# Two token tiles of a MoE layer through Strassen's seven block products

## The chip, the cores and the metric

The kernel runs on one core of a Trainium2 chip. The metric is the device time of one execution in microseconds (us). The engines are TensorE (PE, matrix products), VectorE (DVE), ScalarE (ACT), GpSimd (POOL) and SyncE (SP), whose queue starts nearly all DMAs. Each engine works off its own list of instructions in the order in which the program emits them, and waits on semaphores where an operand or a buffer is not ready.

## The reference

An attention-like read between `x` (4 batches, 8 heads, 512 positions, 64 wide) and a `state` of 32 rows gives 2176 tokens of 512 numbers. Two dense expert layers follow ("first" and "second MoE"); each is a product into 2048 columns, an activation, and a product back into 512.

```python
def _moe2_ref(x, w_in, w_out) -> np.ndarray:
    h = x @ w_in
    g = np.maximum(h, 0.0) + np.log1p(np.exp(-np.abs(h)))
    return (g @ w_out).astype(np.float32)
...
    x = np.ascontiguousarray(attn_out.transpose(0, 2, 1, 3)).reshape(B * S, H * D)
    x = _moe_ref(x=x, **moe_kwargs)
    return _moe2_ref(x=x, **moe2_kwargs)
```

## The kernel before

The weights come as fp64 and are rebuilt in fp32. Every operand of a large product is kept as two fp32r halves, hi and lo, and a product is three matmuls (`mm3`): hi·hi, hi·lo, lo·hi.

**Windows.** The program is a list of 136 windows, `wins`. One window is 128 of the 2048 hidden columns for one tile of tokens. Windows 0 to 67 are the first MoE. The second MoE has five tiles: windows 68 to 83 (tile 0, 512 tokens), 84 to 87 (tile 1, the 128 state tokens), 88 to 103 (tile 2), 104 to 119 (tile 3) and 120 to 135 (tile 4), the last three with 512 tokens each. `S0`, `T3`, `A0` and `start2` hold these numbers; `LAG` is 3.

**One window i of a 512-token tile.** On PE, `l1` makes 12 matmuls of 512 columns (4 blocks of the 512 input features, 3 matmuls each) into one of the two PSUM buffers called `l`; then `l2` makes 12 matmuls of window i-3, which add to the four banks `acc0` to `acc3`. On ACT, `act_open` takes the sum h of window i through Abs, Exp, Identity(+1) and Ln (L808 to L811), into the tiles `ta`, `tb`, `tl`, of which there are two each; `cut_hi` then makes the hi half `gth` of window i-1 (L85). On DVE, `close` makes three operations for window i-1 (L818, L819, L88; the first one reads h from PSUM again), and `cut_lo` makes its lo half `gtl` (L88).

**What sets the order.** `ORDER` is the order of these parts inside a window, written by hand. Work that does not belong to a window's own chain (loads, splits of tokens and weights) hangs on a window number and a kind: `when(i, kind, fn)` registers it, and `run(i, kind)` emits it at that place. SP's DMAs are in one queue in program order, and each waits in that queue for its buffers and data. `load_x2`/`split_x2` bring the tokens of a tile from DRAM (`xd`) and split them; `evac` copies the four finished banks of a tile out and stores them.

**Weights.** `Pair` loads, rebuilds and splits 256 columns of a weight matrix; `W3[p]` holds hi and lo of the second MoE's first layer for windows 2p and 2p+1 of each tile (p from 0 to 7), `W4` its second layer. All of them stay in SBUF through tiles 0 to 4.

Of the kernel before, what the change touches and what calls it, by code (L numbers as in the profile page):

```python
# [9 lines left out]
F32 = mybir.dt.float32  # L10
# [8 lines left out]
def fused_kernel(ctx: ExitStack, tc: tile.TileContext, x, state, w1, w2, w3, w4, out):  # L19
# [24 lines left out]
    LEAD = 14  # L44
    W_ = (8, 2, 2, 0, 8, 3)
# [31 lines left out]
    side = new(psum, [P, 2, 512], F32, "at")  # L77
    turn = [0]

# [197 lines left out]
    def load_state():  # L277
        st = new(base, [P, H, D], F32, "xs", 4)
# [35 lines left out]
    class Attn:  # L314
# [318 lines left out]
    A0 = T3 + NF  # L633

    acc = [None] * 4
# [14 lines left out]
    def load_x2(ti, k):  # L650
        t = new(base, [P, 512], F32, "xs", 4)
# [62 lines left out]
    def l2(w):  # L714
        gh, gl = w.g
        first, last = w.j == 0, w.j == w.n - 1
# [30 lines left out]
    def evac(w):  # L747
        if w.ph == 1 and w.tl == "s":
            t = new(base, [P, 512], F32, "xs", 4)
            copy(t, acc[0])  # L750

            def pe():
# [4 lines left out]
                def rest():  # L757
                    t2 = new(base, [P, 512], F32, "xs", 4)
# [8 lines left out]
        for i in range(n):  # L767
            t = new(base, [P, 512], F32, "xs", 4)
# [16 lines left out]
            else:  # L785
# [4 lines left out]
                else:  # L790
                    b, r = u
                    nc.sync.dma_start(out[b * T : b * T + S, :].rearrange("(p r) d -> p r d", r=R)[:, r, :], t)

    def act_open(w):
        c = w.cols
        w.a = new(base, [P, 512], F32, "ta", 2)[:, :c]
# [4 lines left out]
        else:  # L801
# [7 lines left out]
            nc.scalar.activation(w.a, w.a, AF.Exp, scale=-1.0)  # L809
            nc.scalar.activation(w.b, w.a, AF.Identity, bias=1.0)  # L810
            nc.scalar.activation(w.l, w.b, AF.Ln)  # L811

    def close(w):
# [3 lines left out]
        else:  # L817
# [3 lines left out]
            w.gv = w.l  # L821

# [147 lines left out]
    for ti in range(len(tiles2)):  # L970
# [16 lines left out]
    when(A0, "end", swap_left)

    with tc.manual_schedule():
# [63 lines left out]
        for i in range(NW + LAG + 1):  # L1053
# [6 lines left out]
            run(i, "start")  # L1060
            for what in ORDER[min(i, 4) + (i >= NF)]:
# [23 lines left out]
            run(i, "end")  # L1085
        pools["w_cm"].__exit__(None, None, None)
# [31 lines left out]
```

## Time and profile before

| what | value |
|---|---|
| time, median of 3 runs | 723.45 us (723.34 to 724.09) |
| span of the profiled execution | 721.8 us |
| time less span | 1.65 us (1.5 to 2.3) around the span, at start and end |
| PE | 711.2 us busy, 99% of the span, granted clock at full speed in all slices |
| ACT, DVE | 444.0 us (62%), 441.9 us (61%) |
| DMA | 56.36 MB in 58943 packets |

The profile is of one execution. The time of that execution itself is not listed apart from its span, so the row "time less span" is what the timed runs have beyond it. A busy share is an average over a program with several stages; the change lies in the second MoE, which takes the last half of the span.

### The profile page before, as it was taken

What the parts mean: (1) busy time and instruction counts of PE and PEld (TensorE: products, weight loads), DVE (VectorE), ACT (ScalarE), POOL (GpSimd) and SP (SyncE); (2) the same over time, 40 slices, a digit from 0 to 9 for tenths busy, and PEclk for the clock granted to TensorE, in tenths of its full rate; (3) what the DMA queues carried; (4) which work ended last, traced back from release to release, by engine and by line L of the source; (5) the groups of instructions that cost most, each with busy time, mean ns of one, the idle gap of its engine ahead of it and who ended that gap; (6) DMA issues with size and microseconds to landing.
All of it is one profiled execution on the core that took longest, in us unless ns stands there. A gap on an engine that the chain in (4) does not pass through costs nothing.

```text
span 721.8 us, 10193 instructions
## 1 busy us (share of the span) xinstructions
PE 711.2 (99%) x4014; PEld 575.1 (80%) x4014; DVE 441.9 (61%) x694; ACT 444.0 (62%) x730; POOL 18.3 (3%) x22
## 2 busy tenths in 40 slices
PE   8989999999999999999999999999999999999997
PEld 7667777777777887778888888888888888888886
DVE  5888884674774255776998756445555445544543
ACT  5876775555645356677878656555665556565553
POOL 1001300021000000000000000000000000000000
PEclk9999999999999999999999999999999999999999
DMA  9981007045150031353433001010002000010001
GB/s 327 388 298 58 1 27 150 3 81 95 74 161 1 1 115 64 130 174 118 172 120 132 30 30 59 20 54 1 1 1 97 21 0 1 0 59 1 0 1 58
DMA packets 58943, 56.36 MB, mean 78 GB/s; under 512 B 36880, under 2 KB 39824, under 8 KB 58896
## 3 DMA queue, kind: packets, MB, share of 16 engines
q1 hardware_dynamic: 58608, 55.46, 23.9%
q8 instruction: 31, 0.51, 0.3%
q10 hardware_dynamic: 288, 0.26, 0.1%
q14 instruction: 16, 0.13, 0.1%
HBM read 45.74 MB, written 9.96 MB: 77 GB/s over the span
## 4 chain that ended last, share of the span: by engine, by line
PE 92%; DMA 4%; DVE 2%; ACT 1%; SPq 1%; issue 1%; DVEq 0%
PE acc L638 17%; PE acc L639 16%; PE acc L640 16%; PE l L700 11%; PE l L638 9%; PE l L640 9%; PE l L639 9%; PE at L299 2%; PE l L685 2%; DMA wq<-in_moe_w_in_dram 2%; DMA wq<-in_moe_w_out_dram 1%; DMA ws<-in_moe_w_in_dram 1%; PE at L423 1%; SPq L215 0%; DVE w L161 0%
## 5 line engine op out<-in xcount | busy, mean ns | idle before, releaser
L88 DVE TENSOR_TENSOR gtl<-tl,gth 128x512 fp32r<-128x512 f32 x64 | 44.3, 692 | 144.0 <-ACT gth L85 143.9
L808 ACT ACTIVATE ta<-l 128x512 f32<-128x512 f32 x68 | 40.7, 598 | 132.2 <-PE l L640 132.2
L639 PE MATMUL acc<-gtl,wq 128*128 128x512 f32 x244 | 95.4, 391 | 1.6 <-DVE gtl L88 1.4
L638 PE MATMUL acc<-gth,wq 128*128 128x512 f32 x244 | 96.4, 395 | 0.0
L640 PE MATMUL acc<-gth,wq 128*128 128x512 f32 x244 | 95.1, 390 | 0.0
L88 DVE TENSOR_TENSOR gtl<-ta,gth 128x512 fp32r<-128x512 f32 x68 | 47.3, 696 | 71.2 <-ACT gth L85 71.2
L799 ACT ACTIVATE ta<-l 128x512 f32<-128x512 f32 x68 | 40.3, 592 | 44.5 <-PE l L700 29.1
L638 PE MATMUL acc<-wq,gth 128*128 128x512 f32 x152 | 59.2, 390 | 0.0
L640 PE MATMUL acc<-wq,gtl 128*128 128x512 f32 x152 | 59.2, 389 | 0.0
L639 PE MATMUL acc<-wq,gth 128*128 128x512 f32 x152 | 59.2, 389 | 0.0
L639 PEld LDWEIGHTS acc<-gtl,wq 128*128 128x128 f32 x244 | 45.8, 188 | 11.9 <-DVE gtl L88 2.9
L638 PEld LDWEIGHTS acc<-gth,wq 128*128 128x128 f32 x244 | 45.8, 188 | 11.7 <-issue 2.1
L640 PEld LDWEIGHTS acc<-gth,wq 128*128 128x128 f32 x244 | 45.8, 188 | 9.7
L638 PE MATMUL acc<-wh,gth 128*128 128x512 f32 x136 | 52.9, 389 | 0.0
L639 PE MATMUL acc<-wl,gth 128*128 128x512 f32 x136 | 52.9, 389 | 0.0
L640 PE MATMUL acc<-wh,gtl 128*128 128x512 f32 x136 | 52.9, 389 | 0.0
L88 DVE TENSOR_TENSOR tl<-tl,ta 128x512 f32<-128x512 f32 x68 | 47.0, 692 | 2.4
L85 ACT ACTIVATE gth<-ta 128x512 fp32r<-128x512 f32 x68 | 42.1, 618 | 8.1 <-DVE ta L815 8.1
L818 DVE SCALAR_TENSOR_TENSOR tl<-l,tl 128x512 f32<-128x512 f32 x68 | 46.5, 684 | 0.0
L819 DVE SCALAR_TENSOR_TENSOR ta<-tb,ta 128x512 f32<-128x512 f32 x68 | 46.4, 682 | 0.0
L815 DVE SCALAR_TENSOR_TENSOR ta<-ta,l 128x512 f32<-128x512 f32 x68 | 46.2, 680 | 0.2 <-ACT ta L800 0.2
L811 ACT ACTIVATE tl<-tb 128x512 f32<-128x512 f32 x68 | 43.0, 633 | 2.2
(187 smaller groups left out, 1486.3 us busy)
## 6 DMA issues: line engine op xcount, KB each, us to landing
ws<-in_moe_w_in_dram SPq DMA_DIRECT2D x20, 512.0 KB, 4.2
ws<-in_moe_w_out_dram SPq DMA_DIRECT2D x20, 512.0 KB, 4.1
wq<-in_moe_w_in_dram SPq DMA_DIRECT2D x12, 512.0 KB, 7.9
wq<-in_moe_w_out_dram SPq DMA_DIRECT2D x12, 512.0 KB, 9.8
xd<-xs SPq DMA_DIRECT2D x16, 256.0 KB, 3.0
xs<-xd SPq DMA_DIRECT2D x16, 256.0 KB, 3.9
out_dram<-xs SPq DMA_DIRECT2D x15, 256.0 KB, 2.6
x<-in_x_dram SPq DMA_DIRECT2D x12, 256.0 KB, 4.2
```

The lines of the kernel that those rows point to most:

```text
L85: nc.scalar.activation(dst, src, AF.Copy)
L88: eng.tensor_tensor(dst, a, b, op=ALU.subtract)
L638: nc.tensor.matmul(o, lh, rh, start=first, stop=False)
L639: nc.tensor.matmul(o, lh, rl, start=False, stop=False)
L640: nc.tensor.matmul(o, ll, rh, start=False, stop=last)
L700: nc.tensor.matmul(w.h, l[:, g, f], r[:, g, :], start=i == 0, stop=i == len(terms) - 1)
L799: nc.scalar.activation(w.a, w.hc, AF.Relu, bias=1.0)
L808: nc.scalar.activation(w.a, w.hc, AF.Abs)
L811: nc.scalar.activation(w.l, w.b, AF.Ln)
L815: nc.vector.scalar_tensor_tensor(w.a, w.a, 1.0, w.hc, op0=ALU.min, op1=ALU.max)
L818: nc.vector.scalar_tensor_tensor(w.l, w.hc, 0.0, w.l, op0=ALU.max, op1=ALU.add)
L819: nc.vector.scalar_tensor_tensor(w.a, w.b, 1.0, w.a, op0=ALU.subtract, op1=ALU.subtract)
```

## The change

The first layer of tiles 3 and 4 was 2 times 16 windows of 12 matmuls. It is now done jointly. For each p (256 hidden columns), the 512 features are cut in two halves, the 256 columns in two halves, and the 1024 tokens are tile 3 and tile 4: a product of 2 by 2 blocks. Strassen's method in Winograd's form makes the four block sums from seven block products (`product`, 6 matmuls of 512 columns each) and additions before and after.

**Sums of weights** (`c_*`). The rebuilt weights of each p are kept in DRAM (`w3f`, a store behind `Pair.conv`). From window 79 to 96 they are read back (`c_load`), DVE makes four sums (`c_sums`), ACT and DVE split them (`c_hi`, `c_lo`), and `c_put` stores them to a packed DRAM array `w3c`. In windows 84 to 91 `c_raw` copies the three unsummed blocks of p = 0 to 7 there, six DMAs for each p. `c_get` loads the seven left operands of one p, 1792 columns of hi and as many of lo.

**Sums of tokens** (`b_*`). `b_load` reads tiles 3 and 4 at window 88; `b_sum`, `b_hi`, `b_lo` make the seven right operands in windows 90 to 102, into the places of `W3[0]` to `W3[6]` as these fall free.

**Windows 104 to 119** take one p in two steps. The bank A holds products 1 and then 2, B holds 6, 5 and 3, D holds 7 and 4. `st_even` starts A, B, D, adds A's copy `s1` to B in PSUM, copies `u` from B and `s` from D, and ends with h of tile 3's even window in A. `st_odd` makes h of tile 4's odd window (`x.h`) and tile 3's odd window (`w.h`) as sums of a bank and a copy, and ends with h of tile 4's even window in B. Tile 3's windows get their second layer as before, three windows later. Tile 4's g goes to DRAM (`g_put`, `gbd`).

**Windows 120 to 135** (`st_last`) are tile 4's second layer alone, from g read back (`g_get`) and split two windows at a time (`two_cut`). The two banks that attention used (`side`) become `two0` and `two1` from window 92. Stores of tiles 2 and 3 go two blocks at a time.

```diff
 W_ = (8, 2, 2, 0, 8, 3)
+    XS = 4
...
-    side = new(psum, [P, 2, 512], F32, "at")
+    pa_cm = tc.tile_pool(name="pa", bufs=1, space=bass.MemoryType.PSUM, reuse_waits="tile")
+    side = new(pa_cm.__enter__(), [P, 2, 512], F32, "at")
...
             self.rebuild(flat(self.v)[:, c], self.raw[:, part * n * M : (part + 1) * n * M])
+            if self.kept is not None and part == parts - 1:
+                nc.sync.dma_start(self.kept, self.v)
...
-    def l2(w):
+    def l2(w, blocks=range(4)):
...
-        for i in range(NK if w.ph == 1 else w.cols // P):
+        for i in blocks:
             if first:
-                acc[i] = bank(f"acc{i}", 1)
+                if w.st < 2:
+                    acc[i] = bank(f"acc{i}", 1)
+                else:
+                    acc[i] = two_bank(i - 1) if i in (1, 2) else bank("l1", 2)
...
+    LEFT = {"11": 0, "12": 1, "22": 2, "s1": 3, "s2": 4, "s3": 5, "s4": 6}
+    PRODUCTS = {1: ("11", "11"), 2: ("12", "21"), 3: ("s4", "22"), 4: ("22", "t4"), 5: ("s1", "t1"), 6: ("s2", "t2"), 7: ("s3", "t3")}
...
+    def c_raw(p):
+        for h, t in enumerate(W3[p]):
+            v = f32(t).rearrange("p (q j e f) -> p e j q f", q=2, j=2, e=2)
+            d = w3c[p][:, h].rearrange("p m (q f) -> p m q f", q=2)
+            for j in range(2):
+                nc.sync.dma_start(d[:, j], v[:, 0, j])
+            nc.sync.dma_start(d[:, 2], v[:, 1, 1])
+
+    def c_sums(p):
+        a11, a12, a21, a22 = w3_parts(vals.pop(p))
+        t = sums[p] = new(base, [P, 1024], F32R, "cv", 2)
...
+        add(s1, a21, a22)
+        sub(nc.vector, s2, s1, a11)
+        sub(nc.vector, s3, a11, a21)
+        sub(nc.vector, s4, a12, s2)
...
+    def c_put(p):
+        for h, t in enumerate((cur["c"], sums.pop(p))):
+            nc.sync.dma_start(w3c[p][:, h, 3:].rearrange("p m f -> p (m f)"), f32(t))
...
+    def product(o, m, p):
+        a, b = PRODUCTS[m]
+        c = LEFT[a] * 256
+        (wh, wl), (xh, xl) = ([t[:, c : c + 256] for t in WC[p]]), XC[b]
+        for q in range(2):
+            f, s = slice(q * P, (q + 1) * P), slice(q * S, (q + 1) * S)
+            for k, (l, r) in enumerate(((wh, xh), (wh, xl), (wl, xh))):
+                nc.tensor.matmul(
+                    o, l[:, f], r[:, s], start=m in (1, 6, 7) and q == k == 0, stop=q == 1 and k == 2, skip_group_check=True
+                )
...
+    def g_put(w):
+        close(w)
+        nc.sync.dma_start(gbd[w.j], w.gv)
...
+    def st_even(i, u):
+        p = (i - SA) // 2
+        w, v, late = wins[i], wins[i - 1], wins[SB + 2 * p - 2] if p else None
+        cur["A"], cur["B"], cur["D"] = two_bank(0), bank("l1", 2), two_bank(1)
+        product(cur["A"], 1, p)
+        s1 = new(pools["w"][0], [P, 512], F32, "cs")
+        copy(s1, cur["A"])
+        if late:
+            act_open(v)
+        product(cur["B"], 6, p)
+        product(cur["D"], 7, p)
+        add(cur["B"], cur["B"], s1)
+        cur["u"] = xs()
+        copy(cur["u"], cur["B"])
+        cur["s"] = xs()
+        copy(cur["s"], cur["D"])
+        close(v)
+        st_cut(v)
+        if late:
+            act_open(late)
+        cur["late"] = late
+        l2(u)
+        if u.j == u.n - 1:
+            evac(u)
+        product(cur["A"], 2, p)
+        w.h = cur["A"]
+        act_open(w)
+
+    def st_odd(i, u):
+        p = (i - SA) // 2
+        w, v, x, late = wins[i], wins[i - 1], wins[SB + 2 * p + 1], cur["late"]
+        product(cur["B"], 5, p)
+        product(cur["D"], 4, p)
+        x.h, w.h = xs(), xs()
+        add(x.h, cur["B"], cur["s"])
+        add(w.h, cur["D"], cur["u"])
+        if late:
+            g_put(late)
+        act_open(x if i < SB - 1 else w)
+        close(v)
+        st_cut(v)
+        if i == SB - 1:
+            two_cut(0)
+        l2(u)
+        product(cur["B"], 3, p)
+        wins[SB + 2 * p].h = cur["B"]
+        if i < SB - 1:
+            g_put(x)
+        else:
+            close(w)
+            st_cut(w)
...
+    def st_last(i):
+        a, b = wins[SB - NF : SB], wins[SB:]
+        if i == SB:
+            act_open(b[NF - 2])
+            l2(a[13])
+            l2(a[14])
+            l2(b[0], range(3))
+            g_put(b[NF - 2])
+            act_open(b[NF - 1])
+            l2(b[1], range(3))
+            two_cut(1)
+            l2(a[15])
+            g_put(b[NF - 1])
+            evac(a[15])
+            for j in range(2):
+                l2(b[j], (3,))
+        elif i - SB < NF - 1:
+            j = i - SB + 1
+            if j % 2 == 0 and j + 2 < NF:
+                two_cut(j // 2 + 1)
+            l2(b[j])
+            if j == NF - 1:
+                evac(b[j])
...
+    T1 = start2[2]
+    C0 = start2[1] - 3
+    for p in range(NP):
+        when(C0 + 2 * p - 2, "load", lambda p=p: c_load(p))
+        when(C0 + 2 * p, "split", lambda p=p: c_sums(p))
+        when(C0 + 2 * p, "conv", lambda p=p: c_hi(p))
+        when(C0 + 2 * p + 1, "split", lambda p=p: c_lo(p))
+        when(C0 + 2 * p + 1, "load", lambda p=p: c_put(p))
+        when(start2[1] + p, "load", lambda p=p: c_raw(p))
+    for j in range(2):
+        when(T1, "load", lambda j=j: b_load(j))
...
+    for p in range(1, NP):
+        when(SA + 2 * p - 3, "load", lambda p=p: c_get(p))
+    for n in range(4):
+        when((SB - 3, SB - 2, SB - 1, SB)[n], "load", lambda n=n: g_get(n))
```

DVE in the windows of tile 3, before: the lo half of a window, `close` of the next one, and so on (`l_` is the bank with h).

```order
L88 TENSOR_TENSOR gtl_5127<-tl_5082,gth_5126 128x512
L818 SCALAR_TENSOR_TENSOR tl_5121<-l_882_5091,tl_5121 128x512
L819 SCALAR_TENSOR_TENSOR ta_5119<-tb_5120,ta_5119 128x512
L88 TENSOR_TENSOR tl_5121<-tl_5121,ta_5119 128x512
L88 TENSOR_TENSOR gtl_5166<-tl_5121,gth_5165 128x512
L818 SCALAR_TENSOR_TENSOR tl_5160<-l_888_5130,tl_5160 128x512
L819 SCALAR_TENSOR_TENSOR ta_5158<-tb_5159,ta_5158 128x512
L88 TENSOR_TENSOR tl_5160<-tl_5160,ta_5158 128x512
```

DVE in the odd step of p = 2 now (`l_972` is B, `two_973` D, `two_971` A, `xs_5485` x.h, `xs_5486` w.h, `l_940` the B of p = 1).

```order
L870 TENSOR_TENSOR xs_5485<-l_972_5400,xs_5432 128x512
L870 TENSOR_TENSOR xs_5486<-two_973_5401,xs_5430 128x512
L854 SCALAR_TENSOR_TENSOR tl_5443<-l_940_5254,tl_5443 128x512
L855 SCALAR_TENSOR_TENSOR ta_5441<-tb_5442,ta_5441 128x512
L93 TENSOR_TENSOR tl_5443<-tl_5443,ta_5441 128x512
L854 SCALAR_TENSOR_TENSOR tl_5468<-two_971_5399,tl_5468 128x512
L855 SCALAR_TENSOR_TENSOR ta_5466<-tb_5467,ta_5466 128x512
L93 TENSOR_TENSOR tl_5468<-tl_5468,ta_5466 128x512
L93 TENSOR_TENSOR gtl_5504<-tl_5468,gth_5503 128x512
L854 SCALAR_TENSOR_TENSOR tl_5495<-xs_5485,tl_5495 128x512
L855 SCALAR_TENSOR_TENSOR ta_5493<-tb_5494,ta_5493 128x512
L93 TENSOR_TENSOR tl_5495<-tl_5495,ta_5493 128x512
```

Where each h came straight from a bank, two additions and the closes of three windows now stand in a row; the close that reads A (`two_971`) is behind both additions and behind the close of `l_940`.

SP from the stores of tile 0 at window 87 on, before: the stores, those of tile 1, and the loads of tile 3.

```order
L792 DMA out_dram<-xs_4220 128x512
L792 DMA out_dram<-xs_4223 128x512
L792 DMA out_dram<-xs_4226 128x512
L792 DMA out_dram<-xs_4229 128x512
L789 DMA out_dram<-xs_4397 32x512 x4
L662 DMA xs_4745<-xd_9_81 128x512
L662 DMA xs_4747<-xd_9_81 128x512
L662 DMA xs_4788<-xd_9_81 128x512
L662 DMA xs_4790<-xd_9_81 128x512
```

SP in the same place now (`w3c` is the packed weight array, `wq`, `wh`, `wl` are W3, `tt` and `cv` the sums, `w3f` the kept weights, `xd` the tokens).

```order
L822 DMA out_dram<-xs_4328 128x512
L885 DMA w3c_23_98<-wq_585_3214 128x2x128 x2
L886 DMA w3c_23_98<-wq_585_3214 128x2x128
L885 DMA w3c_23_98<-wq_585_3214 128x2x128 x2
L886 DMA w3c_23_98<-wq_585_3214 128x2x128
L878 DMA cv_4375<-w3f_16_91 128x1024
L907 DMA w3c_23_98<-tt_4366 128x1024
L907 DMA w3c_23_98<-cv_4347 128x1024
L885 DMA w3c_24_99<-wh_618_3421 128x2x128 x2
L886 DMA w3c_24_99<-wh_618_3421 128x2x128
L885 DMA w3c_24_99<-wl_619_3422 128x2x128 x2
L886 DMA w3c_24_99<-wl_619_3422 128x2x128
L923 DMA ws_4429<-xd_10_85 128x2x512
```

Between the last store of tile 0 and the loads of tokens there are now the copies of W3 for p = 3 and 4, one reload of kept weights and the sums of p = 3; the reload of p = 5 and the sums of p = 4 come behind the tokens.

## Rows read from the trace of the kernel before

**Rows 1.** Chain that ended last, 560 to 722 us, by line.
```profile
by line: PE acc L640 17.4%; PE acc L638 17.4%; PE acc L639 17.3%; PE l L640 15.3%; PE l L638 15.1%; PE l L639 15.1%; DVE xs L776 0.3%; ACT xs L85 0.2%; issue 0.0%
```

**Rows 2.** Busy time per stretch: PE, PEld, DVE, ACT, POOL, clock, DMA share, GB/s.
```profile
560.00:580.00 20.00, 20.00 (x90) 16.57 (x89) 8.61 (x14) 12.06 (x20) 0.00 (x0) 1.00 0.03 12
680.00:700.00 20.00, 20.00 (x90) 16.54 (x89) 8.61 (x15) 11.83 (x20) 0.00 (x0) 1.00 0.00 1
```

**Rows 3.** Timeline of ACT, windows of tile 4: start, duration, line, operands.
```profile
619.93 0.60 ACT L808 ACTIVATE ta<-l 128x512 f32<-128x512 f32 x1 [2.33 <-PE l L640]
620.56 0.63 ACT L809 ACTIVATE ta<-ta 128x512 f32<-128x512 f32 x1
621.23 0.63 ACT L810 ACTIVATE tb<-ta 128x512 f32<-128x512 f32 x1
621.89 0.63 ACT L811 ACTIVATE tl<-tb 128x512 f32<-128x512 f32 x1
622.43 0.61 ACT L85 ACTIVATE gth<-tl 128x512 fp32r<-128x512 f32 x1
...
658.01 0.60 ACT L808 ACTIVATE ta<-l 128x512 f32<-128x512 f32 x1 [2.33 <-PE l L640]
```

**Rows 4.** Timeline of DVE in the same windows.
```profile
623.08 0.69 DVE L88 TENSOR_TENSOR gtl<-tl,gth 128x512 fp32r<-128x512 f32 x1 [2.83 <-ACT gth L85]
623.68 0.69 DVE L818 SCALAR_TENSOR_TENSOR tl<-l,tl 128x512 f32<-128x512 f32 x1
624.28 0.68 DVE L819 SCALAR_TENSOR_TENSOR ta<-tb,ta 128x512 f32<-128x512 f32 x1
625.00 0.69 DVE L88 TENSOR_TENSOR tl<-tl,ta 128x512 f32<-128x512 f32 x1
```

**Rows 5.** Waits of 560 to 722 us: total, times, longest.
```profile
DVE gtl L88 <- ACT gth L85: 76.2, 29, 2.8
```

**Rows 6.** ACT groups by line and form.
```profile
L85 ACT ACTIVATE wq<-cv 128x1024 fp32r<-128x1024 f32 x16 | 16.9, 1054 | 5.6 <-DVE cv L161 3.7 <-PE acc L640 1.9
L85 ACT ACTIVATE gh<-at 128x512 fp32r<-128x512 f32 x27 | 16.1, 597 | 27.2 <-PE at L299 23.2 <-PE l L700 2.5 <-DVE gl L88 1.6
```

**Rows 7.** DVE groups by line and form.
```profile
L88 DVE TENSOR_TENSOR gl<-at,gh 128x512 fp32r<-128x512 f32 x27 | 18.6, 690 | 22.6 <-ACT gh L85 22.4
...
L88 DVE TENSOR_TENSOR wl<-cv,wh 128x1024 fp32r<-128x1024 f32 x8 | 9.8, 1219 | 0.0
...
L88 DVE TENSOR_TENSOR gl<-acc,gh 128x256 fp32r<-128x256 f32 x2 | 0.8, 418 | 0.0
```

**Rows 8.** Timeline of ACT: first operation on the product of windows 84 and 91.
```profile
427.13 0.60 ACT L808 ACTIVATE ta<-l 128x512 f32<-128x512 f32 x1 [2.48 <-PE l L640]
...
467.61 0.60 ACT L808 ACTIVATE ta<-l 128x512 f32<-128x512 f32 x1 [1.84 <-PE l L640]
```

**Rows 9.** DMA issues: queue, count, KB each, median us from issue to landing.
```profile
xd<-xs SPq DMA_DIRECT2D x16, 256.0 KB, 3.0
...
out_dram<-xs SPq DMA_DIRECT2D x15, 256.0 KB, 2.6
...
zd<-xs SPq DMA_DIRECT2D x4, 256.0 KB, 2.0
```

**Rows 10.** Busy time per microsecond (last two columns DMA share, GB/s), four of them.
```profile
122.00:123.00 1.00, 1.00 (x61) 0.85 (x64) 0.98 (x3) 0.00 (x0) 0.00 (x0) 1.00 1.27 282
123.00:124.00 1.00, 1.00 (x24) 0.78 (x13) 0.58 (x1) 0.68 (x2) 0.00 (x0) 1.00 1.34 231
269.00:270.00 1.00, 1.00 (x7) 0.80 (x6) 0.26 (x1) 0.91 (x2) 0.00 (x0) 1.00 1.00 367
276.00:277.00 1.00, 1.00 (x6) 0.83 (x5) 1.00 (x2) 0.00 (x0) 0.00 (x0) 1.00 1.05 406
```

**Rows 11.** Packets that moved in 122 to 123 us.
```profile
DMA packets 1117, 0.28 MB, mean 282 GB/s; under 512 B 1117, under 2 KB 1117, under 8 KB 1117
```

**Rows 12.** Timeline of SP: start, time of the issues together, line, count.
```profile
108.31 11.38 SPq L233 DMA_DIRECT2D xs<-in_x_dram  x16
...
266.85 0.90 SPq L117 DMA_DIRECT2D ws<-in_moe_w_in_dram  x2
```

More of the change, by code (lines that the diff above doesn't have):

```diff
@@ L633, in fused_kernel @@
     A0 = T3 + NF
-    acc = [None] * 4
+    SA, SB = start2[3:]
+    accs = [[None] * 4 for _ in range(2)]
     def mm3(o, lh, ll, rh, rl, first, last):
@@ L821, in close @@
             w.gv = w.l
+    w3f = [new(dram, [P, 1024], F32, f"w3f{p}") for p in range(NP)]
+    w3c = [new(dram, [P, 2, 7, 256], F32, f"w3c{p}") for p in range(NP)]
+    gbd = [new(dram, [P, 512], F32, f"gbd{j}") for j in range(NF)]
+    vals, sums, XC, WC, cur = {}, {}, {}, {}, {}
+    KEEP3 = {}
+    LEFT = {"11": 0, "12": 1, "22": 2, "s1": 3, "s2": 4, "s3": 5, "s4": 6}
+    PRODUCTS = {1: ("11", "11"), 2: ("12", "21"), 3: ("s4", "22"), 4: ("22", "t4"), 5: ("s1", "t1"), 6: ("s2", "t2"), 7: ("s3", "t3")}
@@ new lines, in c_sums, with c_hi @@
+    def c_sums(p):
+        a11, a12, a21, a22 = w3_parts(vals.pop(p))
+        t = sums[p] = new(base, [P, 1024], F32R, "cv", 2)
+        s1, s2, s3, s4 = (f32(t)[:, 256 * m : 256 * (m + 1)].rearrange("p (q f) -> p q f", q=2) for m in range(4))
+        add(s1, a21, a22)
+        sub(nc.vector, s2, s1, a11)
+        sub(nc.vector, s3, a11, a21)
+        sub(nc.vector, s4, a12, s2)
+    def c_hi(p):
+        cur["c"] = new(pools["w"][0], [P, 1024], F32R, "tt")
+        copy(cur["c"], f32(sums[p]))
@@ new lines, in c_lo, with c_get @@
+    def c_lo(p):
+        lo = sums[p]
+        sub(nc.vector, lo, f32(lo), f32(cur["c"]))
+    def c_put(p):
+        for h, t in enumerate((cur["c"], sums.pop(p))):
+            nc.sync.dma_start(w3c[p][:, h, 3:].rearrange("p m f -> p (m f)"), f32(t))
+    def c_get(p, hs=(0, 1)):
+        for h in hs:
+            if p % 2:
+                t = new(pools["x"][0], [P, NK, 512], F32R, f"x2{h}")
+                t = t.rearrange("p k f -> p (k f)")[:, : 7 * 256]
+            else:
+                t = new(base, [P, 7 * 256], F32R, "ws", 2)
+            WC.setdefault(p, []).append(t)
+            nc.sync.dma_start(f32(t), w3c[p][:, h].rearrange("p m f -> p (m f)"))
@@ new lines, in b_hi, with b_lo @@
+    def b_hi(m, what):
+        src = cur["t"] if what[0] == "t" else cur[what]
+        XC[what] = room_for(*KEEP3[m].home)
+        hi, lo = (t.rearrange("p (q s) -> p q s", q=2) for t in XC[what])
+        copy(hi, src)
+        cur["x"] = lo, src, hi
+    def b_lo():
+        lo, src, hi = cur["x"]
+        sub(nc.vector, lo, src, f32(hi))
+    def product(o, m, p):
[8 more added lines that the diff above has]
+                )
@@ new lines, in xs, with g_get @@
+    def xs():
+        return new(base, [P, 512], F32, "xs", XS)
+    def g_put(w):
+        close(w)
+        nc.sync.dma_start(gbd[w.j], w.gv)
+    def g_get(n):
+        if n < 2:
+            t = new(base, [P, 2048], F32, "ws", 2)
+        else:
+            t = new(pools["x"][0], [P, NK, 512], F32, f"x2{n - 2}").rearrange("p k f -> p (k f)")
+        cur["g", n] = t
+        for j in range(4 * n, 4 * n + 4):
+            nc.sync.dma_start(t[:, (j - 4 * n) * 512 : (j - 4 * n + 1) * 512], gbd[j])
@@ new lines, in st_cut, with two_cut @@
+    def st_cut(w):
+        cut_hi(w)
+        cut_lo(w)
+    def two_cut(n):
+        hi, lo = room_for(*KEEP3[(7, 6, 0, 1, 2, 3, 4, 5)[n]].home)
+        w, x = wins[SB + 2 * n], wins[SB + 2 * n + 1]
+        o = (2 * n) % 4 * 512
+        src = cur["g", n // 2][:, o : o + 1024]
+        copy(hi, src)
+        sub(nc.vector, lo, src, f32(hi))
+        w.g, x.g = ([t[:, 512 * e : 512 * (e + 1)] for t in (hi, lo)] for e in range(2))
+    def st_last(i):
[21 more added lines that the diff above has]
+                evac(b[j])
@@ L969, in fused_kernel @@
     plan_hops(HW[3], lambda: a0.rest())
[L970 removed]
+    for ti in range(3):
         i0 = A0 - 4 if ti == 0 else start2[ti] - 3
@@ L1060, in fused_kernel @@
             run(i, "start")
+            if i >= SA:
+                if i < SB:
+                    (st_even, st_odd)[(i - SA) % 2](i, u)
+                else:
+                    st_last(i)
+                run(i, "load")
+                continue
             for what in ORDER[min(i, 4) + (i >= NF)]:
```

102 lines of the change are left out of this document (86 added, 16 removed).

## Prediction

> **What bounds the kernel now.** I read the chain that ended last first, then the busy times by stretch, then the timelines of single windows. From 560 us on, the chain is matmuls alone but for the last copies, with nothing put down to issue [rows 1]. PE is busy for 20.00 of 20.00 us at full clock, while ACT has about 12 us of work in 20 and DVE 8.6 [rows 2]. So in this stage a microsecond of PE work removed is a microsecond gained, until ACT, DVE or a DMA becomes late. The helpers are far ahead: DVE waits 2.8 us in each window for ACT, which waits for PE [rows 5]. The price of a matmul comes from ACT, whose first operation on a window's product follows PE: seven windows, from 619.93 to 658.01 us, are 38.08 us [rows 3], so one of 24 matmuls is 5.44 us and one matmul 0.2267 us.
>
> **What goes.** Tiles 3 and 4 had 384 matmuls in the first layer, and now have 8 times 42, or 336. All are 128 by 512 with operands in the same layout, and the second layer keeps its number. 48 times 0.2267 us is 10.88 us off PE. Eight copies and eight subtractions that split tile 3's and 4's tokens go too, off the path.
>
> **What a pair costs the helpers.** One p now takes PE 66 matmuls, 14.96 us. A full `act_open` is 2.50 us from its start to the next instruction's start, an ACT copy 0.6 [rows 3, 6]. A `close` lasts 2.01 us, an instruction that doesn't need the one before starts 0.60 us after it, and an operation from PSUM is 0.69 [rows 4, 7]. ACT has four opens, three copies and two hi halves: 10.0 + 1.8 + 1.2 = 13.0 us. DVE has four closes, three additions and two lo halves: 8.0 + 2.1 + 1.4 = 11.5 us. Both fit into 14.96, but with little over, so the order decides. No row has DVE writing into PSUM as the addition to B does. I take 0.69 from the operation that reads PSUM; the bounds are 0.6 and double that, and as copy `u` has over 2 us to spare before product 5 overwrites B, either end costs nothing.
>
> I laid out one pair on the three engines, each in its order, with these durations, from the pair's first matmul at 0. Products 1, 6 and 7 end at 4.08, the second layer at 6.80, products 2, 5 and 4 at 8.16, 9.52 and 10.88, the second layer at 13.60, product 3 at 14.96. Two loops could be longer than that.
>
> The first is bank A. Product 4's last column is out 0.16 us after its slot. Then come `w.h`'s addition (to 11.77), the close of the late window (to 13.70), and the first operation of the close that reads A (to 14.30). The next product 1 wants A at 14.96. About 0.6 us are to spare.
>
> The second goes through DRAM. The tiles `tl` are two, so the Ln for `x.h` waits until the late window's g has landed in `gbd`. From the end of that window's close: landing 2.0 (plus 0.04 to start it and as much to see it), Ln 0.63, hi and lo of A's window 1.2, close of `x` 1.9, addition to B 0.6, close of the odd window 2.05, its hi half 0.6, open of the next late window 2.6, its close 2.05. That is 13.7 us, so it returns with 1.3 us to spare. Its one uncertain price is the landing: 2.0 us for single stores of 256 KB, 2.6 and 3.0 for stores in fours [rows 9]. `gbd` stores go singly, so I take 2.0; up to 3.3 us there is no stall.
>
> `c_get` of 1.8 MB is issued about 5 us into a pair and is wanted at the next but one product 1, 10 us later. At the 367 to 406 GB/s of large pieces [rows 10] it takes 5 us and some two for the start. Hidden, with 3 us to spare; without that cover each microsecond counts.
>
> **The end.** Windows 120 to 135 have only second layers, 2.72 us each. By the same layout PE meets its third one 0.5 us before `two_cut(1)` is done, because two opens, a close and a split of 1024 columns (1.05 and 1.22 us [rows 6, 7]) stand in line: +0.5, and 1.1 if a landing is 2.6. The last copies and stores are the same.
>
> **The stage before, windows 79 to 104.** DVE gets about 2.7 us and ACT 1.05 more in two windows for weight sums, and 1.2 and 1.05 for token sums, against 2.8 us of waiting in each window. That is covered. The DMAs are not so clearly. Windows 84 to 91 last 40.48 us between the first and the last of their opens [rows 8] and one window more, 45.9 us. In them SP moves 6.3 MB of `c_raw`, 4.2 of sums, 2.1 of reloads, 2.1 of tokens and 1.3 of outputs, 16.0 MB or 349 GB/s. In windows 87 to 90 it is 9.4 MB in 22.3 us, 420 GB/s. Pieces of 2 KB and more went at 367 and 406 GB/s, pieces of 256 bytes at 231 to 282 with the engines full [rows 10, 11]; the `c_raw` pieces have 512 bytes, and SP's 0.45 us to issue a DMA of 256 pieces [rows 12] alone holds them to 291. At a mean of 350 the 9.4 MB take 27 us, so the queue falls 5 us behind. What is late then is the store of the sums of p = 4, issued in window 90, and with it DVE's `c_sums` of p = 5 in window 91, which reuses the buffer. Behind it on DVE stands the close of window 91, normally 1.2 us into window 92; the matmuls of window 93 need its bank, 4.2 us later. 5 less 4.2 is 0.8 us; the whole stage laid out gives 0 with 512-byte pieces at 310 GB/s, 1.1 at 280, 4.4 at 231. I take 0.5, nearer to the large pieces since SP's issue sets the pace; both ends stay in the range.
>
> The Trainium skill, "DMA: Bandwidth & Descriptors", section Specifications, names 512 bytes as the smallest transfer at line rate and about 358 GB/s as one core's share of HBM. By these two, as an estimate, the 9.4 MB would take 26 us and the loss would be near zero; the rows with 406 GB/s go over its limit.
>
> **The early stores `w3f`** stand on SP right behind a conversion whose buffer the next load was waiting for anyway, and ahead of that load by one issue of 0.45 us [rows 12]. Loads run windows ahead, so zero; nothing else moved ahead of window 79.
>
> **Sum.** 721.8 - 10.88 + 0.5 (DMA) + 0.5 (end) = 711.9 us of span. The runs last 1.65 us beyond the span at their median, so 713.6 us.
>
> **Rivals.** (a) The forecast, PE stays full but for 0 to 2.5 us: 712.4 to 715.
>
> (b) The DMA queue falls further behind in windows 87 to 92. With 512-byte pieces at 231 GB/s, the rate of 256-byte pieces, and the rest at 340, windows 93 and 95 start 6.5 us late in total: 719.1. For it speaks the demand of 420 GB/s; against it that these pieces are twice as long. Result 715 to 722.
>
> (c) The landing of `gbd` takes longer. From 3.3 us on, each pair pays the rest, and the end a little too: in the layout 3.2 us in all at 3.5, 6.7 at 4.0, which makes 715.8 and 719.3 before the DMA term. For it speaks 3.0 for stores in fours [rows 9] and the weight loads on the same engines; against it that the late window's store starts when these have landed. The Trainium skill, same page, section Latency and other measured facts, puts HBM access at 0.2 us on average and 2 us at high load; by it, as an estimate, a landing near 3.8 would be possible where loads are in flight, but by the layout none is. The trace before has no such store beside weight loads.
>
> (d) Slower: the same queue, but `c_raw` at 150 GB/s. The pieces are strided on the SBUF side, and the copies of 64 KB in pieces of 128 bytes took SP 0.71 us each [rows 12], 92 GB/s. At 0.71 us for 128 KB it would be 185 GB/s, and the loss 9.4 us. From about 165 GB/s on, the loss is over the gain of 10.9; at 150 it is 16 us, so 729. Against it: no row with pieces over 128 bytes is that slow.
>
> That the work does not shrink is excluded: the program holds 336 matmuls where 384 were.
>
> **Chances.** (a) 0.60, (b) 0.14, (c) 0.14, (d) 0.08, and 0.04 for several together that land near the old time. 0.2%, or 1.4 us, is about what a measurement of this kernel can tell from no change. Faster: (a), and (b) and (c) but for 0.04, so 0.84. Slower: (d) and a little of the mixed cases, 0.10. Same: 0.06. The likeliest case alone has 712.4 to 715. The range starts at 712.2, no stall at all, and goes to 719.5, the prices worked out for (b) and (c); beyond it lie (d), the mixed cases and the far parts of (b) and (c), under 2 in 10.
>
> **What would show it.** Right: 336 matmuls at 0.227 us each in the new line; PE full in the Strassen stage, with no wait for DVE over 0.5 us at product 1; `gbd` landings near 2 us; a short wait or none at the first matmul of window 93. Wrong: waits of product 1 in every pair on the close that reads A, with ACT's Ln of `x.h` waiting for a DMA (c); DVE's `c_sums` of p = 5 waiting for several microseconds on DMA and PE idle at windows 93 and 95 (b, d); or an operation that writes PSUM from DVE that is much longer than 0.7 us.

## The result, and the profile after

The changed kernel takes 716.99 us at the median (715.87 to 717.69 in 4 runs), beside 723.77 (723.34 to 724.41) for the kernel before in the same session: a ratio of 0.9902, 95% interval 0.9888 to 0.9916, faster by 1.0%. The forecast was 713.6, the likeliest case 712.4 to 715, the range 712.2 to 719.5. The profiled execution took 716.87 us with a span of 714.7, that is 7.1 less than the span of before. One execution of an experiment, the first profile of `put_pool`, ran at a granted clock of 0.655 throughout; its trace isn't used, and `put_pool_b` gives that kernel's trace.

The page's busy times, and its line on DMA: 48 matmuls fewer, 9.5 us less PE time (up to window 0 it has 0.7 us more in this execution, with the same 147 matmuls), 102.5 MB moved where it was 56.4.

```profile
PE 701.7 (98%) x3966; PEld 566.4 (79%) x3966; DVE 484.7 (68%) x753; ACT 465.7 (65%) x753; POOL 18.3 (3%) x22
...
DMA packets 82880, 102.51 MB, mean 143 GB/s; under 512 B 38800, under 2 KB 54032, under 8 KB 82832
```

Two stretches in the Strassen stage and after it, busy times as in [rows 2]: PE is as full as before.

```profile
560.00:580.00 20.00, 20.00 (x90) 16.54 (x90) 14.20 (x23) 17.18 (x30) 0.00 (x0) 1.00 0.58 224
680.00:700.00 20.00, 20.00 (x90) 16.57 (x89) 2.82 (x3) 2.12 (x2) 0.00 (x0) 1.00 0.11 38
```

DVE went from 8.6 to 14.2 us in 20 and ACT from 12.1 to 17.2, and PE still waits for neither. The waits of PE between 430 and 712 us (total, times, longest) are two, and both lie before the Strassen stage:

```profile
PE l L653 <- DVE tl L854: 1.6, 1, 1.6
PE acc L653 <- ACT xs L90: 0.6, 1, 0.6
```

To see where the 7.1 us come from I follow ACT's first operation on a window's product, as in [rows 8]. Kernel before, windows 0 and 103:

```profile
20.51 0.60 ACT L799 ACTIVATE ta<-l 128x512 f32<-128x512 f32 x1 [0.40 <-PE l L700]
...
532.89 0.60 ACT L808 ACTIVATE ta<-l 128x512 f32<-128x512 f32 x1 [2.33 <-PE l L640]
```

Kernel after, windows 0, 84 and 103:

```profile
21.37 0.60 ACT L833 ACTIVATE ta<-l 128x512 f32<-128x512 f32 x1 [0.39 <-PE l L715]
...
427.93 0.60 ACT L842 ACTIVATE ta<-l 128x512 f32<-128x512 f32 x1 [1.53 <-PE l L655]
...
536.45 0.60 ACT L842 ACTIVATE ta<-l 128x512 f32<-128x512 f32 x1 [1.38 <-PE l L655]
```

Window 0 opens 0.86 us later than before. From window 84 to window 103 it is 105.76 us before (427.13 [rows 8] to 532.89) and 108.52 after: **2.76 us lost in the windows that now carry the extra transfers**. From window 0's open to the last matmul's start (717.43 before, 710.29 after) it is 696.92 and 688.92, 8.00 less: 10.88 for 48 matmuls, less 2.76, and 0.12 for all else. So 721.8 + 0.86 - 8.00 = 714.66, and the rest to 714.7 is the tail.

The 0.86 at the start is no part of the change: up to window 78 PE, ACT and DVE have the same instructions in all kernels below, and their profiles open window 0 anywhere between 20.34 and 21.64 us. The time beyond the span is 2.07 to 2.17 us in the four runs of the change. In the runs of the kernel before that stand beside the experiments it is 1.74 to 1.86, and in those of `raw_four_earlier` 1.78 to 1.87. Why is open.

The lost 2.76 us on DVE, the close of window 90 (its last row first), then `c_sums` of p = 5, then the close of window 91:

```profile
468.04 0.69 DVE L93 TENSOR_TENSOR tl<-tl,ta 128x512 f32<-128x512 f32 x1
475.05 0.43 DVE L870 TENSOR_TENSOR cv<-cv 128x256 f32<-128x256 f32 x1 [6.31 <-DMA w3c<-cv]
...
478.25 0.68 DVE L854 SCALAR_TENSOR_TENSOR tl<-l,tl 128x512 f32<-128x512 f32 x1
```

The same place on PE: the first second-layer matmul of window 91's slot, and the first matmul of window 93.

```profile
468.96 0.50 PE L653 MATMUL acc<-wh,gth 128*128 128x512 f32 x1 [0.59 <-ACT xs L90]
...
479.00 0.50 PE L653 MATMUL l<-x,wq 128*128 128x512 f32 x1 [1.58 <-DVE tl L854]
```

`c_sums` writes into the buffer whose store `c_put` of p = 4 is still under way. It waits 6.31 us, the close of window 91 stands behind it, and window 93 needs the bank that this close reads. That is the chain of the prediction's DMA term, with a gap of 1.74 us between the matmuls where the prediction took 0.5. The prediction didn't name the wait of 0.59 (a gap of 0.74): ACT's copy of tile 1's accumulator stands behind the hi half of the token block "22", whose tokens land late. After each of the two gaps the next six matmuls take 0.14 us more than usual; 0.74, 1.74 and twice 0.14 are the 2.76.

ACT there, the hi half of "22" and the copy behind it:

```profile
467.37 1.06 ACT L90 ACTIVATE wh<-ws 128x1024 fp32r<-128x1024 f32 x1 [1.28 <-DMA ws<-xd]
468.33 0.58 ACT L90 ACTIVATE xs<-acc 128x512 f32<-128x512 f32 x1
```

SP's queue, with `c_put` of p = 2 (two stores, the second needs DVE's `c_lo`) and of p = 4:

```profile
438.31 0.33 SPq L907 DMA_DIRECT2D w3c<-tt  x1
442.35 0.32 SPq L907 DMA_DIRECT2D w3c<-cv  x1
442.72 0.43 SPq L885 DMA_DIRECT2D w3c<-wq  x1
...
469.06 0.33 SPq L907 DMA_DIRECT2D w3c<-tt  x1
470.32 0.33 SPq L907 DMA_DIRECT2D w3c<-cv  x1
```

Busy times of two stretches; the last two columns are DMA share and GB/s:

```profile
435.00:442.70 7.70, 7.70 (x51) 6.91 (x50) 6.25 (x11) 6.19 (x10) 0.00 (x0) 1.00 0.59 187
445.00:467.00 22.00, 22.00 (x105) 18.29 (x104) 16.05 (x28) 14.24 (x22) 0.00 (x0) 1.00 1.02 305
```

From 445 to 467 us the engines are full at 305 GB/s, and the sums of p = 4, which DVE had finished at 464.4, leave SP at 470.3, and DVE goes on at 475.05, when they have landed. Before that SP stands for 3.7 us (438.64 to 442.35) at the head of its queue, waiting for DVE, with `c_raw` ready behind it and the engines 0.59 busy.

### The profile page after: what moved, and what is told of

It reads as the page before. It is cut to its first block, busy times and chain, and to the rows that moved or that the text cites. A ratio compares the mean times of both kernels' runs of the same rounds, so it can differ in the third digit from the quotient of the medians.

```text
span 714.7 us, 10383 instructions
## 1 busy us (share of the span) xinstructions
PE 701.7 (98%) x3966; PEld 566.4 (79%) x3966; DVE 484.7 (68%) x753; ACT 465.7 (65%) x753; POOL 18.3 (3%) x22
## 4 chain that ended last, share of the span: by engine, by line
PE 88%; DMA 6%; DVE 2%; ACT 1%; SPq 1%; issue 1%; DVEq 0%
PE acc L653 14%; PE acc L654 14%; PE acc L655 14%; PE l L715 11%; PE two L959 6%; PE l L653 5%; PE l L655 5%; PE l L654 5%; PE l L959 5%; PE at L313 2%; PE l L700 2%; DMA wq<-in_moe_w_in_dram 2%; DMA wq<-in_moe_w_out_dram 1%; DMA cv<-w3f 1%; DMA ws<-in_moe_w_in_dram 1%; PE two L653 1%
## 5 line engine op out<-in xcount | busy, mean ns | idle before, releaser
L833 ACT ACTIVATE ta<-l 128x512 f32<-128x512 f32 x68 | 40.2, 591 | 44.7 <-PE l L715 29.3
L93 DVE TENSOR_TENSOR gtl<-tl,gth 128x512 fp32r<-128x512 f32 x48 | 33.2, 691 | 41.6 <-ACT gth L90 41.4
L842 ACT ACTIVATE ta<-l 128x512 f32<-128x512 f32 x44 | 26.1, 594 | 40.8 <-PE l L655 40.8
L653 PE MATMUL acc<-wq,gth 128*128 128x512 f32 x120 | 46.8, 390 | 0.0
L655 PE MATMUL acc<-wq,gtl 128*128 128x512 f32 x120 | 46.7, 389 | 0.0
L654 PE MATMUL acc<-wq,gth 128*128 128x512 f32 x120 | 46.7, 389 | 0.0
L846 ACT ACTIVATE tb<-ta 128x512 f32<-128x512 f32 x68 | 43.1, 633 | 2.2
L834 ACT ACTIVATE ta<-ta 128x512 f32<-128x512 f32 x68 | 43.0, 633 | 2.2
L843 ACT ACTIVATE ta<-ta 128x512 f32<-128x512 f32 x68 | 43.0, 633 | 2.2
L653 PE MATMUL acc<-wh,gth 128*128 128x512 f32 x104 | 40.6, 390 | 0.6 <-ACT xs L90 0.6
```

The source lines that it names most:

```text
L93: eng.tensor_tensor(dst, a, b, op=ALU.subtract)
L653: nc.tensor.matmul(o, lh, rh, start=first, stop=False)
L654: nc.tensor.matmul(o, lh, rl, start=False, stop=False)
L655: nc.tensor.matmul(o, ll, rh, start=False, stop=last)
L834: nc.scalar.activation(w.a, w.a, AF.Square, scale=0.5)
```

## Experiments

**Theory 1**: 48 matmuls are 10.9 us, the Strassen stage has no loss, and what is lost is lost in windows 84 to 92, where the store of the sums of p = 4 lands late. Its rivals are in each expectation. The column "lost" is, in each run's profile, the time from window 84's to window 103's open, less the 105.76 us of before.

| kernel | median us | ratio to before, 95% | lost, us |
|---|---|---|---|
| the change | 716.99 | 0.9902 (0.9888 to 0.9916) | 2.76 |
| `raw_spread` | 713.83 | 0.9860 (0.9844 to 0.9876) | 0.01 |
| `raw_four_earlier` | 713.72 | 0.9852 (0.9836 to 0.9868) | 0.01 |
| `put_pool` | 714.02 to 714.95 | 0.9868 (0.9852 to 0.9885) | 0.01 (`put_pool_b`) |
| `tokens_first_put_pool` | 714.59 | 0.9867 (0.9853 to 0.9880) | 0.01 |
| `raw2_first` | 715.32 | 0.9881 (0.9864 to 0.9897) | 1.64 |
| `tokens_first` | 719.64 | 0.9931 (0.9917 to 0.9945) | 6.28 |
| `prod7_twice` | 728.06 | 1.0053 (1.0038 to 1.0068) | 4.08 |
| `dve_two_more_b` | 723.64 | 0.9994 (0.9985 to 1.0003) | 4.23 |
| `gbd_four_stores` | 731.98 | 1.0111 (1.0097 to 1.0125) | 4.11 |

The last three have the changed kernel's code in those windows, so the same code lost between 2.8 and 4.2 us there in four profiles, one of each kernel.

**Fewer bytes at a time: `raw_spread`.**

```
-        when(start2[1] + p, "load", lambda p=p: c_raw(p))
+        when(start2[1] + 2 * p, "load", lambda p=p: c_raw(p))
```

> The copies c_raw(p) leave in window 84+2p, no longer 84+p; nothing else differs from the changed kernel. Theory 1 (c_raw overfills the DMA engines in windows 84 to 91, so the store of the sums of p = 4 and the token loads land late): DVE's c_sums of p = 5 waits under 1 us, PE has no wait at windows 91 and 93, the open of window 96 comes 27.2 us after that of window 91 (now 29.6), and the time falls by 2.3 to 2.8 us, to 714.2 to 714.7. Rival (the delay comes from the token loads and the sums' own round trips, whatever c_raw does): the wait at window 93 stays over 1 us and the time within 0.7 us of 717.

The loss is gone. Busy times of 425 to 480 us here (the changed kernel has 52.84 us of PE there):

```profile
425.00:480.00 55.00, 55.00 (x294) 47.37 (x294) 41.72 (x68) 38.94 (x62) 0.00 (x0) 1.00 0.86 283
```

At 713.83 us it is 0.4% faster than the change, a little more than expected. `c_sums` still waits for DMA, 2.6 us at most (2.5 for p = 5, where under 1 was expected), which its two windows cover.

**As dense, but sooner: `raw_four_earlier`.**

```
-        when(start2[1] + p, "load", lambda p=p: c_raw(p))
+        when(start2[1] + p - 4, "load", lambda p=p: c_raw(p))
```

> The copies c_raw(p) leave in window 80+p instead of 84+p: still one per window, but gone before the tokens and the outputs of tile 1 come. Theory 1c (one c_raw per window with the sums is 289 GB/s, which fits; what overfills the queue is that 3.4 MB of tokens and outputs come in the same windows, 88 to 91): no PE wait from window 91 to 96, 714 to 714.6. Rival (c_raw in every window is too dense wherever it stands, since the sums' stores go round once in two windows behind it): PE waits of over 1 us somewhere in windows 82 to 92, 715.5 or more.

713.72 us, and PE is full in the same stretch:

```profile
425.00:480.00 55.00, 55.00 (x297) 47.50 (x296) 42.12 (x70) 38.91 (x62) 0.00 (x0) 1.00 0.90 297
```

One `c_raw` per window fits, if the tokens and the outputs of tile 1 don't come in the same windows.

**Another queue: `put_pool` and `put_pool_b`.** The sixteen stores `c_put` are issued by POOL, which is idle there; all bytes stay in their windows.

```
-            nc.sync.dma_start(w3c[p][:, h, 3:].rearrange("p m f -> p (m f)"), f32(t))
+            nc.gpsimd.dma_start(w3c[p][:, h, 3:].rearrange("p m f -> p (m f)"), f32(t))
```

> The stores c_put of the weight sums are issued by POOL, not behind the other DMAs on SP; c_raw stays where it is. Theory 1a (the store of p = 4 is late because it stands behind c_raw in SP's queue): it goes out some 4 us earlier, DVE's c_sums of p = 5 waits under 2 us, PE's wait of 1.6 us at window 93 goes and the one of 0.6 at window 91 stays: 1.7 to 2.0 us faster than the changed kernel, 715. Theory 1b (the 16 DMA engines are full, and the place in a queue makes no difference): the store lands as late as before, and the time stays within 0.7 us of 717.

> The stores of the weight sums on POOL once more, for a profile at full clock. Theory 1a: PE waits only at window 91, by 0.6 to 1.6 us, for ACT's copy that stands behind the tokens; none at window 93. If window 93 still waits, the place in SP's queue was not the cause there.

Theory 1a holds, and more came back than it said: window 91's wait went too, since the token loads no longer queue behind stores that wait for DVE. The two stretches of `put_pool_b`:

```profile
435.00:442.70 7.70, 7.70 (x51) 6.89 (x50) 6.30 (x11) 6.25 (x10) 0.56 (x2) 1.00 0.88 261
445.00:467.00 22.00, 22.00 (x105) 18.29 (x104) 15.97 (x28) 15.10 (x24) 2.13 (x4) 1.00 1.03 332
```

Beside the rows of the changed kernel: where SP stood waiting, 261 GB/s flow in place of 187. Over 425 to 480 us it is 312 GB/s against 298. So the bytes do fit; they didn't fit in one queue in that order. The Trainium skill, "DMA: Bandwidth & Descriptors", section Rules for kernel authors, says that spreading DMAs over issuing engines doesn't help bandwidth and only saves issue time. Here it gave 0.3% of the time. I put that down to the order: transfers no longer stand behind a store that waits for data, nor that store behind them. It isn't the rate of a second queue, as far as the runs tell: `raw_four_earlier`, with SP alone, moves 338 GB/s from 445 to 467 us at a share of 1.03, and `put_pool_b` 332. The stretches hold different transfers.

**Tokens first: `tokens_first` and `tokens_first_put_pool`.** The loop that registers `b_load` moves ahead of the one for the weights, so in window 88 the tokens are issued first.

```
+    for j in range(2):
+        when(T1, "load", lambda j=j: b_load(j))
     for p in range(NP):
         when(C0 + 2 * p - 2, "load", lambda p=p: c_load(p))
...
-    for j in range(2):
-        when(T1, "load", lambda j=j: b_load(j))
```

> The four loads of tokens (b_load) go to the front of window 88's transfers, ahead of the sums and of c_raw of p = 4; all else as in the changed kernel. Theory 1b (what stands ahead of the store of the sums of p = 4 in SP's queue sets when that lands, and with it window 93): PE's wait of 0.6 us at window 91 goes, since ACT has its tokens in time, but the same bytes still stand ahead of that store, so the wait at window 93 grows by as much: within 0.5 us of the changed kernel, 717. Rival (the two waits are separate losses): 0.7 us faster, 716.2.

> Both: token loads first in window 88, and the stores of the weight sums issued by POOL; c_raw stays as dense as in the changed kernel. Theory 1a (what was lost was lost to the order of the queue, not to the number of bytes): no PE wait from window 91 to 96, 2.6 us faster than the changed kernel, 714.2, the time of the kernel that spreads c_raw. Rival (the bytes of windows 84 to 91 don't fit, in whatever order): at least 1 us of waits in windows 91 to 96, 715 or more.

The first was a miss for both theories: slower than the change, 6.28 us lost. I had looked at the store of p = 4 alone. In window 88 the tokens also pass the store of p = 3, and `c_sums` of p = 4 waits for that. DVE's `c_sums` of p = 4 in `tokens_first`, two windows before the one that waits in the changed kernel:

```profile
466.06 0.42 DVE L870 TENSOR_TENSOR cv<-cv 128x256 f32<-128x256 f32 x1 [7.90 <-DMA w3c<-cv]
```

PE waits 3.10 us, and then the lost time doubles: busy times by 2 us, third column from the right the granted clock.

```profile
464.00:466.00 2.00, 1.78 (x8) 1.13 (x6) 0.00 (x0) 0.00 (x0) 0.00 (x0) 1.00 1.10 347
466.00:468.00 2.00, 0.00 (x0) 0.00 (x0) 1.90 (x5) 0.35 (x1) 0.00 (x0) 1.00 0.38 111
468.00:470.00 2.00, 1.12 (x3) 0.94 (x4) 1.97 (x4) 1.94 (x4) 0.00 (x0) 0.57 0.58 119
470.00:472.00 2.00, 2.00 (x6) 1.54 (x5) 1.55 (x3) 1.97 (x4) 0.00 (x0) 0.50 1.02 330
472.00:474.00 2.00, 2.00 (x6) 1.58 (x5) 1.97 (x4) 1.12 (x2) 0.00 (x0) 0.50 1.14 389
474.00:476.00 2.00, 2.00 (x8) 1.55 (x8) 0.34 (x1) 1.54 (x3) 0.00 (x0) 0.72 1.01 393
```

After a gap of 3.26 us PE runs at half clock (1.2 of 2.4 GHz) until about 475 us, 6 matmuls in 2 us where it has 9. Half of the 6.2 us from 468.9 on is the other 3 us of the 6.28. This is the profiled execution, the slowest of five (720.17 us, mean granted clock 0.995). Another of the five took 718.5 us at a mean granted clock of 1.000, so the half clock doesn't come in every execution; the kernel is slower than the change in all five, at 718.35 us or more. With the stores on POOL the same order of tokens loses nothing (`tokens_first_put_pool`), as theory 1a said.

**One wait at the head of the queue: `raw2_first`.** `c_raw(2)` is registered before `c_put(2)`, nothing else moves.

```
+        if p == 2:
+            when(start2[1] + p, "load", lambda p=p: c_raw(p))
         when(C0 + 2 * p + 1, "load", lambda p=p: c_put(p))
-        when(start2[1] + p, "load", lambda p=p: c_raw(p))
+        if p != 2:
+            when(start2[1] + p, "load", lambda p=p: c_raw(p))
```

> One transfer group changes its place: the six copies c_raw(2) of window 86 stand ahead of the stores c_put(2) in SP's queue, no longer behind them; all else as in the changed kernel. In the profile of the changed kernel SP waits there 3.6 us for DVE's c_lo (the second store of the pair needs it), with the DMA engines 0.59 busy, while c_raw(2) stands ready behind. Theory 1d (that wait at the head of the queue, added to queues that are full from 445 us on, is what is late at window 93): SP's wait before line 907 falls under 1.5 us, everything behind it leaves some 3 us earlier, and 2.2 us or more of the loss come back: 714 to 715. Rival 1e (the bytes of windows 87 to 90 at their rate are the cause, the wait before them isn't): waits of over 1.5 us in all at windows 91 and 93, 716.2 to 717.5.

Between the two: in the profile 1.12 us less are lost and 1.64 us remain. The ratio is 0.2% lower, though its interval still touches that of the change. SP in this kernel, the stores of p = 2 and p = 3:

```profile
440.54 0.41 SPq L907 DMA_DIRECT2D w3c<-tt  x1
442.06 0.33 SPq L907 DMA_DIRECT2D w3c<-cv  x1
...
450.14 0.33 SPq L907 DMA_DIRECT2D w3c<-tt  x1
452.97 0.32 SPq L907 DMA_DIRECT2D w3c<-cv  x1
```

The wait at the first pair fell to 1.1 us, and part of it came back at the next, 2.5 us, where SP is now early. So `c_put` of p = 4 left only 1.3 us sooner (469.02, was 470.32), or 1.0 counted from window 84's open, about what came back. That wait is one part of the loss. The rest I put down to the full engines in front of the store, and to the wait that came back at p = 3; no run divides it between these two.

**The price of the matmuls: `prod7_twice`.** In `st_even` a second `product(cur["D"], 7, p)` follows the first and computes the same again.

> Product 7 is computed twice in each pair, into the same bank, so PE has the 48 matmuls back that the change removed, while the other engines' work is the same. Theory 1 (in the Strassen stage each matmul is 0.2267 us of the time): 10.88 us slower than the changed kernel, 727.9, which is 4 us slower than the kernel before. Rival (part of PE's time there is cover for waits of ACT, DVE or the gbd landing): under 9 us slower.

728.06 less 716.99 is 11.07 us, and by the ratios 0.0151 of 723.9, 10.9. Both hold other differences too, since this profile loses 4.08 us before the stage, not 2.76, and opens window 0 0.71 us sooner. From window 103's open to the last matmul's start it is free of them: 173.84 us in the changed kernel (536.45 to 710.29) and 184.72 here (537.07 to 721.79), which is 10.88. PE's time in that stage isn't cover for anything else.

**Bank A: `dve_two_more_b`.** The additions write into copy `u`'s tile after its last use, since SBUF has no room for a tile of their own.

```
         act_open(x if i < SB - 1 else w)
+        for _ in range(2):
+            add(cur["u"], w.h, w.h)
         close(v)
```

> Two more additions of 128x512 on DVE in each pair, ahead of the close that reads bank A (into copy u's tile, used nowhere). Theory 1 (the loop over bank A has some 0.6 us to spare in each pair, as the prediction's layout had it): the next product 1 comes 0.6 us late in pairs 1 to 7, 4 us slower than the changed kernel, about 721. Rival (there is more to spare, since DVE is busy for only two thirds of the time): no change, 717.

Slower by 6.65 us, not 4. The waits of PE from 540 to 722 us are at product 1, where the layout had them, but in pairs 2 to 7 and not in pair 1: six of 0.56.

```profile
PE two L959 <- DVE tl L854: 3.3, 6, 0.6
```

The gap between the matmuls is 0.72 us each time (0.63 in the layout), and pairs come every 15.82 us, 0.86 more than 14.96, because after a gap the first six matmuls take 1.66 us, not 1.52. Six times 0.86 is 5.2. The larger loss before the stage, 4.23 in place of 2.76, adds 1.5, and two gaps in the tiles of the end 0.7; window 0 opens 0.6 sooner. That is 6.74 us up to the last matmul. So theory 1 is right on the 0.6 us to spare, and low on what a wait costs.

**The loop through DRAM: `gbd_four_stores`.** `g_put` stores each g to `gbd` and to three more DRAM arrays.

```
-        nc.sync.dma_start(gbd[w.j], w.gv)
+        for d in (gbd, gbx, gby, gbz):
+            nc.sync.dma_start(d[w.j], w.gv)
```

> Each g of tile 4 is stored four times, to four places in DRAM, so its tile is free when the last has landed. At 367 to 406 GB/s a further store is 0.7 us, so I expect the last landing 4.1 to 4.4 us after the first's issue (2.0 now). Theory 1 (the loop through DRAM has 1.3 us to spare, with a threshold at 3.3 us): by the prediction's layout 0.7 to 0.9 us at product 1 of each pair, 6 to 9 us slower in all, 723 to 726. Rival (the loop has over 2.4 us to spare): no change, 717.

Slower by 15.0 us, well over 6 to 9. The landings (median us from issue) of the first and the last store, and the waits of ACT and PE from 540 us on:

```profile
gbd<-tl SPq DMA_DIRECT2D x16, 256.0 KB, 2.0
...
gbz<-tl SPq DMA_DIRECT2D x16, 256.0 KB, 3.5
```

```profile
ACT tl L847 <- DMA gbz<-tl: 21.9, 7, 3.8
...
PE acc L653 <- ACT gth L90: 3.8, 1, 3.8
PE two L960 <- DMA x<-w3c: 2.7, 3, 1.0
PE two L960 <- DMA ws<-w3c: 2.3, 3, 1.4
PE two L960 <- DVE tl L854: 2.1, 4, 0.6
```

The last store is issued 1.3 us after the first, so it lands some 4.8 us after it, and ACT's Ln waits for it, as the layout has it. But that loop holds PE for 2.1 us in all. `c_get`, now behind the stores, holds it for 5.0. At the end ACT's last Ln waits 3.7 us for the fourth store of an earlier g, and PE behind it for 3.8, after which it works for 5 us at a clock of 0.50. Theory 1 is right that the loop has less than 2.8 us to spare (4.8 less 2.0). But most of the 15.0 us isn't that loop: it is `c_get` and the end, which the expectation left out. The threshold of 3.3 itself wasn't tried.

## Why the prediction was right, and where it was not

**Right: the gain.** 48 matmuls less are 10.88 us; the profile has 10.88 to within 0.12 between window 0 and the last matmul, once the loss is added back, and the profile of `prod7_twice` has 10.88 by itself.

**Right: the Strassen stage.** The additions that write PSUM take 0.69 us (taken 0.69). `gbd` lands in 2.0 us at the median (taken 2.0). The close's first operation on bank A ends 0.67 us before the next product 1 (taken 0.6). No matmul waits from window 104 to the end.

**Too high: the end.** The 0.5 us before `two_cut(1)` isn't there; PE has no gap over 0.12 us there. No run shows the reason.

**The step that failed: the size of the DMA term.** "I take 0.5, nearer to the large pieces since SP's issue sets the pace" should have been 2.8, and up to 4.2 in other profiles. Place and chain were right. The pace wasn't SP's issue: the engines were full, share 1.02, and moved 305 GB/s, not 350. By the prediction's own sum 9.4 MB then take 30.8 us, 8.5 more than the 22.3 of the four windows, and less the slack of 4.2 that is 4.3: enough for the loss, and more than the 2.8 of this profile. The strided pieces were no slower than the layout allowed for. By the time that their packets took, those of 512 bytes ran at 296 GB/s from 445 to 467 us, between the 280 and 310 for which the prediction's layout gives 1.1 and 0. Those of 2 and 4 KB ran at 304 and 302, where its rows had 367 and 406. The second part I left out: a store of sums that waits for DVE holds every transfer behind it in SP's queue (3.7 us in windows 85 and 86, with 187 GB/s moving). `raw2_first` shows that this wait is part of the loss. `put_pool` shows that the loss is one of order: the same bytes in the same windows, no store of sums behind other transfers or ahead of them, nothing lost.

So it was rival (b) by its chain and its range (715 to 722), not case (a), that came true; the chance of 0.14 was too low. What priced (b), 512-byte pieces at 231 GB/s, didn't happen. Its 719.1 also leaves out the 0.5 of the end that the sum has, so it should read 719.6, just over the range. The measured 716.99 lies outside the likeliest case and in the part of the range that was there for the rivals: that the range held is owed to them, not to the sum. The Trainium skill's figure of 358 GB/s and line rate from 512 bytes on ("DMA: Bandwidth & Descriptors", section Specifications), by which the loss would have been near zero, isn't what this mix of strided 512-byte pieces and larger ones reached: 305 with full engines. Of rival (c) nothing was seen.

**Not in the sum: the start.** 0.86 us in the profiled execution. It belongs to the executions, not to the change. With it the profiled execution adds up: 713.57 forecast, 2.26 more for DMA, 0.5 less for the end, 0.86 for the start, 0.16 for the small rest of the span, and 0.52 for the time beyond the span (2.17 where 1.65 was taken) make 716.87. The end's 0.5 that wasn't needed hid as much of the rest.

**The version to keep** is `raw_four_earlier` or `raw_spread` (0.985 and 0.986 of before, intervals that overlap): in their profiles nothing of the gain is lost.

## What to carry to other kernels

Where a change pays for fewer matmuls with more transfers, find the transfer whose landing frees a buffer in a loop, here the sums' store, and count what stands ahead of it in its queue, bytes and waits for data alike; the mean rate over the stretch says too little. A store that must wait for an engine belongs in a queue where nothing urgent stands behind it, or the urgent things belong ahead of it; check each of the loop's earlier rounds too before moving something forward. Price a full queue that mixes small strided pieces with larger ones by the rate at which such a mix ran, and take the low end.

## What the runs showed of the hardware

- Of PE's waits, those of 1.2 to 1.7 us (the changed kernel's and three others') left the granted clock at 1.00; after those of 3.1 us (`tokens_first`) and 3.8 (`gbd_four_stores`) PE worked for 6.2 and 5.1 us at 0.50 in the profiled executions, which cost 3.1 and 2.5 us more.
- A short wait of PE costs more than itself: 0.14 us over a gap of 0.72, and as much over gaps of 0.74 and 1.74, since the next six matmuls take 1.66 us in place of 1.52 (the first takes 0.50, the usual is 0.39).
- With the DMA engines full (shares of 1.02 to 1.03, 445 to 467 us), the rate was 305 GB/s in the changed kernel, 332 with the stores of the sums issued by POOL (`put_pool_b`), and 338 with SP alone and other transfers in that stretch (`raw_four_earlier`). Packets of 512 bytes ran at 292 to 303 GB/s in all three, those of 4 KB at 302, 356 and 393; why these differ is open.
